# Four-layer forward and backward pass: attention's output stage inside the feed-forward loop, queries projected beside keys, backward weights transposed into SBUF

## The chip, the cores and the metric

One core of a Trainium2 chip runs the whole kernel. The metric is device time in microseconds, as the median of several runs; lower is better. A core has five engines with instruction queues of their own: TensorE (PE, matrix products, with a separate weight-load stream PEld), VectorE (DVE), ScalarE (ACT), GpSimd (POOL) and SyncE (SP), which here issues the DMA transfers. Each queue runs in its own order, and semaphores tie them to one another. Products land in PSUM, a small memory of eight banks, from which DVE or ACT must take them.

## The reference

The kernel computes the forward pass of four layers and the gradients for the input and all five weights. Shapes: sequence S = 2048, width D = 512, feed-forward width F = 1376, 32 heads of 16. Layers 0 and 2 are the linear attention A, layers 1 and 3 the gated feed-forward block B, with the same weights in both pairs.

```python
def _A_ref(x, wqkv, wo):                      # phi(t) = where(t>0, t+1, exp(t)) + 1e-6
    q, k, v = split(x @ wqkv)                 # each [32 heads, S, 16]
    pq, pk = phi(q), phi(k)
    kv = einsum("bhsd,bhse->bhde", pk, v)     # summed over the whole sequence
    z = einsum("bhsd->bhd", pk)               # the same
    num = einsum("bhqd,bhde->bhqe", pq, kv)
    den = einsum("bhqd,bhd->bhq", pq, z)[..., None] + 1e-6
    return (num / den).reshape(B, S, D) @ wo

def _B_ref(x, w_gate, w_up, w_down):
    return (sigmoid(x @ w_gate) * (x @ w_up)) @ w_down

x = x + _A_ref(layernorm(x)); x = x + _B_ref(layernorm(x))
x = x + _A_ref(layernorm(x)); x = x + _B_ref(layernorm(x))
```

Outputs are the last x and the gradients of its product with `grad_out`. What matters for the order of work: kv and z need the keys of every position, so no attention output can be computed before the last key; everything after them is independent from tile to tile.

## The kernel before

The sequence is cut into 16 tiles of 128 rows (`NST`), the width into 4 chunks of 128 (`NDC`), the feed-forward width into 11 chunks (the last of 96 rows), worked on in three slices of 512, 512 and 352 columns. The residual stream lives in SBUF in fp32 (`k.xs[st]`). DRAM buffers (`sv_...`) hold what the backward pass will need. The program is written as loops over tiles; a scheduler arranges each engine's queue from it, so a queue's order can differ from the program's.

*Start.* `load_stream` (L93) loads x in bf16, in batches of four tiles, and casts each tile to fp32, alternately on DVE and ACT. The weights follow in the same DMA queue.

*Attention, layers 0 and 2:* `a_fwd` (from L455). The layer norm of a tile (`layernorm_tile`, L290) is bn_stats and bn_aggr on DVE (L293, L295), rstd in two POOL steps (L296, L297), the factor nmr on DVE (L299) and the scaled copy on ACT (L300); four TensorE transposes (L308) and a copy out of PSUM follow. In the key pass, for each tile: project k (four products of 128x512, L484), phi (exp on ACT L490, a minimum L491 and a maximum L492 on DVE) into `pk_all`, and the accumulation of X = h^T phi(k) (L499) one tile later. Then z (L522), kv (L532, from X and the value weights, so v is never computed) and M = kv·wo (L537). In the query pass (`stage_q`), for each tile: project q (L484 again), phi, the product with z on POOL (`prod`, L553), its sum over heads on DVE (`den`, L555), a scalar step (L556), the reciprocal (L557), the normalised query `pqn` (L559, DVE), four transposes and an ACT copy. `stage_y`, four tiles behind (`LA = 4`), multiplies by M (L573), copies the result with ACT (L576) and adds it to x on POOL (L577). MT (L591) is computed and stored at the end, for the backward pass.

*Feed-forward, layers 1 and 3:* `b_fwd` (from L600). For each tile and slice: g (L652) and u (L655), four products each; sigmoid(g) and sigmoid(-g) on ACT (L657, L659); hh = u · sigmoid on DVE (L660); a second product on POOL (L661) for the backward pass; and transposes of the slice before (L617) with ACT copies (L620, L622). One tile behind, `finish` runs 11 products with the down weights (L629), a DVE add to x (L631), and the next layer's norm for that tile (`nxt.stage`), or, in layer 3, a copy of the output (`out_cb`, L191).

*Weights for the backward pass.* `wT_groups` (L336) transposes the weights in groups of four PE transposes with an evacuation on DVE or ACT. The groups run as `extra` at the end of each tile: 34 groups (gate, up, down) in layer 1, 16 (wqkv, wo) in layer 3. All go through a staging tile into DRAM. `load_b_weights` (L205) loads them back ahead of each B layer's backward pass.

*Backward.* `b_bwd_p1` and `a_bwd_p1` walk the layers down, with passes for weight gradients behind them. In layer 3 `GPrep` casts the incoming gradient into `k.xs` (L704, L706) and transposes it. In `a_bwd_p1` the gradient of z is accumulated by small products `dz` (L971) that need `cneg_bf` from POOL (L969).

Of the kernel before, what the change touches and what calls it, by code (L numbers as in the profile page):

```python
# [17 lines left out]
D = 512  # L18
# [32 lines left out]
def kernel(  # L51
# [41 lines left out]
    def load_stream(io, src2d, b):  # L93
        stg_t = io.tile([P, NB, D], BF16, name="io_in")
        if b == 0:
            nc.sync.dma_start(out=stg_t[:, 0, :], in_=src2d[0:P, :])
            nc.sync.dma_start(out=stg_t[:, 1:NB, :],
                              in_=src2d[P:NB * P, :].rearrange("(n p) d -> p n d", p=P))
        else:
            nc.sync.dma_start(out=stg_t[:], in_=dram_batch(src2d, b))  # L100
        for j in range(NB):
            st = b * NB + j
            if j % 2 == 0:
                nc.vector.tensor_copy(k.xs[st][:], stg_t[:, j, :])
            else:
                nc.scalar.copy(k.xs[st][:], stg_t[:, j, :])
        return stg_t
    k.load_stream = load_stream

    def store_stream(io, dst2d, b):  # L110
        stg_t = io.tile([P, NB, D], BF16, name="io_out")
        for j in range(NB):
            st = b * NB + j
            nc.gpsimd.tensor_scalar(stg_t[:, j, :], k.xs[st][:], 1.0, 0.0, ALU.mult, ALU.add)
        nc.sync.dma_start(out=dram_batch(dst2d, b), in_=stg_t[:])
    k.store_stream = store_stream


    k.sv = {}
    for l in range(4):  # L120
# [18 lines left out]
        wgT=dram.tile([F, D], BF16, name="wgT_d"),  # L139
        wuT=dram.tile([F, D], BF16, name="wuT_d"),  # L140
# [11 lines left out]
    k.A_wo = A_wo  # L152
    with tc.tile_pool(name="wfwd", bufs=1) as wfwd:
        k.wqkv = wfwd.tile([P, NDC, 3 * D], BF16, name="wqkv")
        with tc.tile_pool(name="io0", bufs=2) as io:
            load_stream(io, x_in, 0)
            nc.sync.dma_start(out=k.wqkv[:], in_=A_wqkv.rearrange("(c p) j -> p c j", p=P))
            for b in range(1, NST // NB):
                load_stream(io, x_in, b)
# [9 lines left out]
        nc.sync.dma_start(out=k.wd[0:FLAST, NFC - 1, :], in_=B_w_down[(NFC - 1) * P:F, :])  # L169

        with ExitStack() as lctx:
            k.lnres = dict(
                stg=lctx.enter_context(tc.tile_pool(name="ln_stg", bufs=2)),
                hT=lctx.enter_context(tc.tile_pool(name="ln_hT", bufs=4)),
                small=lctx.enter_context(tc.tile_pool(name="ln_small", bufs=6)),
                ps=lctx.enter_context(tc.tile_pool(name="ln_ps", bufs=1, space=PSUM)),
            )
            k.hres = lctx.enter_context(tc.tile_pool(name="ln_hall", bufs=1))
            lns = [FwdLNAll(k, l) if l % 2 == 0 else FwdLN(k, l) for l in range(4)]
            wtg_b, wtg_a = wT_groups(k)  # L180
            a_fwd(k, 0, lns[0], nxt=lns[1])
            with tc.tile_pool(name="wt_stage", bufs=2) as wt_stage:
                b_fwd(k, 1, lns[1], nxt=lns[2], extra=wtg_b, wt_stage=wt_stage)
            a_fwd(k, 2, lns[2], nxt=lns[3])
            ostg = lctx.enter_context(tc.tile_pool(name="out0_stg", bufs=2))
            ocur = {}

            def out_cb(st):
                if st % NB == 0:
                    ocur["t"] = ostg.tile([P, NB, D], BF16, name="out0_t")  # L190
                nc.scalar.copy(ocur["t"][:, st % NB, :], k.xs[st][:])  # L191
                if st % NB == NB - 1:
                    nc.sync.dma_start(out=dram_batch(out0, st // NB), in_=ocur["t"][:])
            with tc.tile_pool(name="wt_stage2", bufs=2) as wt_stage:
                b_fwd(k, 3, lns[3], out_cb=out_cb, extra=wtg_a, wt_stage=wt_stage)
# [5 lines left out]
    with ExitStack() as bctx:  # L201
        wb = bctx.enter_context(tc.tile_pool(name="wbwd", bufs=1))
        k.wb = wb

        def load_b_weights():  # L205
            k.wdT = wb.tile([P, NDC, F], BF16, name="wdT", tag="w_c")
            nc.sync.dma_start(out=k.wdT[:], in_=k.wT["wdT"].rearrange("(c p) f -> p c f", p=P))
            k.wuT = wb.tile([P, NFC, D], BF16, name="wuT", tag="w_a")
            k.wgT = wb.tile([P, NFC, D], BF16, name="wgT", tag="w_b")
            for t_sb, t_d in ((k.wuT, k.wT["wuT"]), (k.wgT, k.wT["wgT"])):  # L210
                nc.sync.dma_start(out=t_sb[:, 0:NFC - 1, :],
                                  in_=t_d[0:(NFC - 1) * P, :].rearrange("(c p) j -> p c j", p=P))
                nc.sync.dma_start(out=t_sb[0:FLAST, NFC - 1, :], in_=t_d[(NFC - 1) * P:F, :])
# [76 lines left out]
def layernorm_tile(k, small, x_t, h_out, rstd_out):  # L290
    nc = k.nc
    stats = small.tile([P, 6], F32, name="ln_stats")
    nc.vector.bn_stats(stats[:], x_t[:])  # L293
# [5 lines left out]
    nc.vector.tensor_scalar(nmr[:], mv[:, 0:1], -1.0, rstd_out, ALU.mult, ALU.mult)  # L299
    nc.scalar.activation(h_out, x_t[:], ACT.Identity, bias=nmr[:], scale=rstd_out)  # L300


def transpose_blocks(k, ps_pool, dst, src_blocks, evac, tag="tp"):
    nc = k.nc
    n = len(src_blocks)
    ps = ps_pool.tile([P, n, P], BF16, name=tag, tag=tag)
    for i, sb in enumerate(src_blocks):
        nc.tensor.transpose(ps[:, i, :], sb, k.ident[:])  # L308
    evac_copy(k, dst, ps[:], evac)
# [26 lines left out]
def wT_groups(k):  # L336
    nc = k.nc
    groups, groups_a = [], []
    cnt = [0]

    def evac(dst, src):
# [4 lines left out]
        cnt[0] += 1  # L346

    for w_sb, wT_d, C in ((k.wg, k.wT["wgT"], F), (k.wu, k.wT["wuT"], F),
                          (k.wqkv, k.wT["wqkvT"], 3 * D), (k.wo, k.wT["woT"], D)):
        ncc = (C + P - 1) // P  # L350
        for cc0 in range(0, ncc, 4):
            ccs = list(range(cc0, min(cc0 + 4, ncc)))
            holder = {}
            for j, cc in enumerate(ccs):
                def g(stage, ps_pool, w_sb=w_sb, wT_d=wT_d, C=C, cc0=cc0, ccs=ccs, j=j, cc=cc, holder=holder):
                    if j == 0:
                        holder["t"] = stage.tile([P, 4, D], BF16, name="wt_st")
                    st_t = holder["t"]
                    r = min(P, C - cc * P)
                    ps = ps_pool.tile([P, NDC, P], BF16, name="hhT_ps")  # L360
                    for rc in range(NDC):
                        nc.tensor.transpose(ps[0:r, rc, :], w_sb[:, rc, cc * P:cc * P + r], k.ident[:])
                    evac(st_t[0:r, j, :], ps[0:r, :, :].rearrange("p a b -> p (a b)"))
                    if j == len(ccs) - 1:
                        nfull = len([c_ for c_ in ccs if min(P, C - c_ * P) == P])
                        if nfull > 0:
                            nc.sync.dma_start(
                                out=wT_d[cc0 * P:(cc0 + nfull) * P, :].rearrange("(n p) d -> p n d", p=P),
                                in_=st_t[:, 0:nfull, :])
                        if nfull < len(ccs):  # L370
                            c_ = ccs[nfull]
                            r_ = C - c_ * P
                            nc.sync.dma_start(out=wT_d[c_ * P:c_ * P + r_, :], in_=st_t[0:r_, nfull, :])
                (groups_a if w_sb is k.wqkv or w_sb is k.wo else groups).append(g)
    for cc in range(NDC):
        holder = {}
        for fs in range(3):
            def g(stage, ps_pool, cc=cc, fs=fs, holder=holder):
                if fs == 0:
                    holder["t"] = stage.tile([P, F], BF16, name="wdt_st")  # L380
                st_t = holder["t"]
                fcs = fchunks_of_slice(fs)
                ps = ps_pool.tile([P, NDC, P], BF16, name="hhT_ps")
# [4 lines left out]
                evac(st_t[:, c0:c0 + w], ps[:].rearrange("p a b -> p (a b)")[:, 0:w])  # L388
                if fs == 2:
                    nc.sync.dma_start(out=k.wT["wdT"][cc * P:(cc + 1) * P, :], in_=st_t[:])  # L390
            groups.append(g)
    return groups, groups_a
# [5 lines left out]
class FwdLN:  # L398
# [7 lines left out]
    def stage(self, st):  # L406
# [7 lines left out]
        layernorm_tile(k, R["small"], k.xs[st], h_t, k.rstd[l][:, st:st + 1])  # L414
# [3 lines left out]
        transpose_blocks(k, R["ps"], hT[:], [h_t[:, c * P:(c + 1) * P] for c in range(NDC)], "vector", tag="ln_tp")  # L418
# [11 lines left out]
class FwdLNAll:  # L430

    def __init__(self, k, l):
        self.k, self.l = k, l
# [3 lines left out]
    def stage(self, st):  # L437
# [3 lines left out]
        R = k.lnres  # L441
        if st == 0:
            self.h_all = k.hres.tile([P, NST, D], BF16, name="h_all")
            self.hT_all = k.hres.tile([P, NST, NDC, P], BF16, name="hT_all")
        h_t = self.h_all[:, st, :]
        layernorm_tile(k, R["small"], k.xs[st], h_t, k.rstd[l][:, st:st + 1])
        transpose_blocks(k, R["ps"], self.hT_all[:, st, :, :], [h_t[:, c * P:(c + 1) * P] for c in range(NDC)],
# [729 lines left out]
```

## Time and profile before

| | us |
|---|---|
| median of 3 runs (1398.99 to 1402.82) | 1399.81 |
| the profiled execution's own time | 1402.44 |
| its span (first to last instruction) | 1400.6 |
| PE busy / DVE / ACT / POOL | 1244.4 / 712.8 / 591.1 / 339.6 |
| mean granted TensorE clock | 0.965 |

The profile shows one execution. In its lines "L652" is a line of the kernel, "128x512" partitions by elements, "x4" the number of instructions in the line. A bracket such as [20.43 <-DMA ssd_ld] is the idle time of that engine before the instruction and what ended it. TensorE instructions are pipelined, so one of 128x512 has a duration of 379 ns while the next follows after 216.

Landmarks on this execution's clock, from its timeline:

| event | us |
|---|---|
| first key projection of layer 0 | 14.0 |
| z of layer 0 complete | 53.9 |
| first g product of layer 1 | 124.9 |
| last y product of layer 1 | 276.4 |
| z of layer 2 complete | 310.4 |
| first g product of layer 3 | 383.3 |
| last y product of layer 3 | 521.1 |
| first transposes of the backward pass | 541.5 |
| end | 1400.6 |

### The profile page before, as it was taken

To read this page: it belongs to the slowest core of one execution; us is meant where nothing else is said; L and a number is where in the kernel's file an instruction comes from. 1 tells how busy PE (TensorE), PEld (TensorE's weight loads), DVE (VectorE), ACT (ScalarE), POOL (GpSimd) and SP (SyncE) were. 2 spreads that over 40 slices of the span, in tenths; PEclk is the share of its full clock that TensorE was granted. 3 is DMA by queue.
4 is the path that set the end of the run, shared out by engine and by line. 5 is a ranking of instruction groups with operands and counts; after the bars stand their busy time and mean duration, and the time that the engine had idled before them with its cause. 6 is when DMAs were issued, how large, how long until landed. Compare 5 with 4: busy or idle time off the path is not lost. (4 is left out here: it accounts for less than half of the span.)

```text
span 1400.6 us, 22220 instructions
## 1 busy us (share of the span) xinstructions
PE 1244.4 (89%) x8506; PEld 720.3 (51%) x8628; DVE 712.8 (51%) x1440; ACT 591.1 (42%) x1092; POOL 339.6 (24%) x500
## 2 busy tenths in 40 slices
PE   5867999896689985999978999999999989996998
PEld 2423555442245542555454557775455745554777
DVE  6694655558853332666476660016555285650211
ACT  7445666634467652444442441134443333520000
POOL 4175444406753330000162000001100441110000
PEclk9988999999899996999999999999999999998999
DMA  8312444421234459755673739887554956559963
GB/s 316 135 61 99 182 183 187 168 105 61 86 146 192 167 187 314 271 176 177 199 224 106 240 100 319 223 224 245 200 187 168 297 155 190 182 142 313 254 159 91
DMA packets 260937, 260.15 MB, mean 186 GB/s; under 512 B 28448, under 2 KB 241376, under 8 KB 260832
## 3 DMA queue, kind: packets, MB, share of 16 engines
q1 hardware_dynamic: 248352, 251.40, 56.1%
q10 hardware_dynamic: 12480, 7.34, 1.9%
q8 instruction: 67, 1.10, 0.3%
q14 instruction: 38, 0.31, 0.1%
HBM read 139.85 MB, written 118.85 MB: 185 GB/s over the span
## 5 line engine op out<-in xcount | busy, mean ns | idle before, releaser
L868 PE MATMUL p_ps<-p_set,p_a 128*128 128x256 bf16 (+1 forms) x1792 | 194.6, 267 | 10.5 <-DVE dw_stg L873 7.4
L868 PEld LDWEIGHTS <-p_a 128*128 128x128 bf16 x1792 | 161.3, 99 | 33.6 <-issue 6.5
L661 POOL TENSOR_TENSOR ssd_t<-hh_t,oms 128x512 bf16<-128x512 bf16 (+1 forms) x96 | 101.7, 1062 | 99.6 <-ACT oms L659 60.1
L765 ACT COPY ddT<-T_ps 128x1024 bf16<-128x1024 bf16 (+1 forms) x96 | 83.2, 867 | 93.1 <-PE T_ps L763 92.9
L683 DVE SCALAR_TENSOR_TENSOR junk<-t_sb,h_ld 128x512 bf16<-128x512 f32 x64 | 45.8, 715 | 139.8 <-ACT t_sb L681 139.7
L685 POOL TENSOR_SCALAR ab<-c 128x2 f32<-128x2 f32 x64 | 12.2, 191 | 384.2 <-DVE junk L683 373.9
L777 PEld LDWEIGHTS <-ddT 128*128 128x128 bf16 (+1 forms) x704 | 65.9, 97 | 68.9 <-issue 10.4
L777 PE MATMUL dh_ps<-wuT,ddT 128*128 128x512 bf16 (+1 forms) x330 | 94.4, 379 | 6.9 <-ACT t_sb L681 3.4
L652 PE MATMUL g_ps<-wg,hT 128*128 128x512 bf16 (+1 forms) x368 | 92.9, 362 | 8.1 <-ACT oms L659 5.2
L681 ACT ACTIVATE t_sb<-dh_ps,rstd_all 128x512 f32<-128x512 f32 x64 | 44.0, 687 | 133.0 <-issue 60.4
L660 DVE TENSOR_TENSOR hh_t<-u_ps,ssd_t 128x512 bf16<-128x512 f32 (+1 forms) x96 | 60.8, 633 | 67.0 <-PE u_ps L655 49.5
L655 PE MATMUL u_ps<-wu,hT 128*128 128x512 bf16 (+1 forms) x384 | 93.0, 361 | 0.0
L795 PE MATMUL dhh_ps<-wdT,gT 128*128 128x512 bf16 x383 | 87.2, 364 | 2.8 <-ACT gT L317 2.8
L797 DVE TENSOR_TENSOR dd_t<-dhh_ps,ssd_ld 128x512 bf16<-128x512 f32 (+1 forms) x96 | 60.5, 630 | 53.9 <-issue 48.7
L484 PE MATMUL mm_ps<-wqkv,hT_all 128*128 128x512 bf16 x249 | 73.0, 409 | 14.2 <-DVE pq_t L492 13.9
L777 PE MATMUL dh_ps<-wgT,ddT 128*128 128x512 bf16 (+1 forms) x352 | 81.3, 379 | 0.0
L898 PE MATMUL p_ps<-p_a,p_set 128*128 128x512 bf16 (+1 forms) x331 | 79.0, 379 | 2.5 <-DMA p_set<-sv_hdd 2.0
L629 PE MATMUL y_ps<-wd,hhT 128*128 128x512 bf16 (+1 forms) x336 | 78.3, 379 | 1.2 <-DVE x L631 0.4
L620 ACT COPY hhT<-hhT_ps 128x512 bf16<-128x512 bf16 (+1 forms) x96 | 49.5, 516 | 57.9 <-PE hhT_ps L617 57.9
L763 PEld LDWEIGHTS <-dd_t 128*128 128x128 bf16 (+1 forms) x704 | 50.7, 100 | 40.6 <-DVE dd_t L797 18.9
L763 PE MATMUL T_ps<-ident,dd_t 128*128 128x128 bf16 (+1 forms) x704 | 66.5, 220 | 3.5 <-DVE dd_t L797 3.2
L553 POOL TENSOR_TENSOR prod<-pq_t,zb 128x512 bf16<-128x512 bf16 x32 | 43.3, 1357 | 93.5 <-DVE pq_t L492 90.1
(193 smaller groups left out, 2250.1 us busy)
## 6 DMA issues: line engine op xcount, KB each, us to landing
p_set<-sv_hdd SPq DMA_DIRECT2D x30, 1024.0 KB, 7.5
sv_ssd<-ssd_t SPq DMA_DIRECT2D x32, 688.0 KB, 3.0
ssd_ld<-sv_ssd SPq DMA_DIRECT2D x32, 688.0 KB, 5.6
sv_hdd<-dd_t SPq DMA_DIRECT2D x32, 688.0 KB, 3.8
sv_hdd<-hh_t SPq DMA_DIRECT2D x32, 344.0 KB, 2.2
h_ld<-sv_h SPq DMA_DIRECT2D x32, 256.0 KB, 3.7
p_a<-sv_h SPq DMA_DIRECT2D x12, 512.0 KB, 6.7
sv_h<-h_all SPq DMA_DIRECT2D x8, 512.0 KB, 3.6
```

The costliest lines, as they stand in the source:

```text
L484: nc.tensor.matmul(ps[:], lhsT=ln.hT_all[:, st, kc, :], rhs=k.wqkv[:, kc, n * D:(n + 1) * D], start=(kc == 0), stop=(kc == NDC - 1))
L629: nc.tensor.matmul(y_ps[:], lhsT=T["hhT"][0:r, fc, :], rhs=k.wd[0:r, fc, :], start=(fc == 0), stop=(fc == NFC - 1))
L652: nc.tensor.matmul(g_ps[:, 0:w], lhsT=hT[:, kc, :], rhs=k.wg[:, kc, c0:c0 + w], start=(kc == 0), stop=(kc == NDC - 1))
L655: nc.tensor.matmul(u_ps[:, 0:w], lhsT=hT[:, kc, :], rhs=k.wu[:, kc, c0:c0 + w], start=(kc == 0), stop=(kc == NDC - 1))
L660: nc.vector.tensor_tensor(hh_t[:, c0:c0 + w], u_ps[:, 0:w], ssd_t[:, 0, c0:c0 + w], ALU.mult)
L661: nc.gpsimd.tensor_tensor(ssd_t[:, 1, c0:c0 + w], hh_t[:, c0:c0 + w], oms[:, 0:w], ALU.mult)
L763: nc.tensor.transpose(tps[0:r, a, i, :], dd[:, a, fc * P:fc * P + r], k.ident[:])
L765: nc.scalar.copy(ddT[:, :, fcs[0]:fcs[0] + nfull, :], tps[:, :, 0:nfull, :])
L777: nc.tensor.matmul(dh_ps[:], lhsT=T["ddT"][0:r, a, fc, :], rhs=wT[0:r, fc, :], start=(i == 0), stop=(i == n_mm - 1))
L795: nc.tensor.matmul(dhh_ps[:, 0:w], lhsT=gT[:, jc, :], rhs=k.wdT[:, jc, c0:c0 + w], start=(jc == 0), stop=(jc == NDC - 1))
L868: nc.tensor.matmul(psv[:, icl, :], lhsT=lhs_all[:, st, ic * P:(ic + 1) * P], rhs=set_t[:, st, 0:W], start=(st == 0), stop=(st == NST - 1))
L898: nc.tensor.matmul(ps[0:r, :], lhsT=st_t[:, st, j * P:j * P + r], rhs=g_all[:, st, :], start=(st == 0), stop=(st == NST - 1))
```

## The change

The key and query passes become one: `kq_fwd` projects k and q for a tile one after the other, takes both exponentials into one tile, and does the minimum for both in one DVE instruction of twice the width. phi(q) of all tiles stays in SBUF (`pq_all`). The transposes of h move from the layer norm into this pass (ACT copies them), the X accumulation runs two tiles behind, and MT is computed right after M. The phi(q) factor is stored tile by tile instead of in batches of four.

The rest of attention moves into the feed-forward loop, `ab_fwd`. `front1` (the product with z, den), `front2` (scalar, reciprocal, pqn) and `front3` (transposes) run three tiles ahead of the feed-forward tile (`FLAG`), `attn_y` and its add two tiles ahead (`YLAG`). The attention add moves from POOL, behind an ACT copy, to DVE, straight from PSUM. Attention's y and the feed-forward's y share one PSUM bank; the transposes of pqn and of h share another.

x stays in bf16 for layer 0 (no casts; the first attention add reads it), and wqkv is loaded in three parts between the batches of x. nmr moves from DVE to POOL. The weight groups change places: 16 (wqkv, wo) run in layer 1, 34 (down, up, gate) in layer 3, and these are evacuated straight into the SBUF tiles that layer 3's backward pass reads, with one store each to DRAM for layer 1's; so layer 3 has no reload. The incoming gradient is read in bf16 where it is used. The `dz` products are issued one tile later in the program.

```diff
 def layernorm_tile(k, small, x_t, h_out, rstd_out):
-    nc.vector.tensor_scalar(nmr[:], mv[:, 0:1], -1.0, rstd_out, ALU.mult, ALU.mult)
+    nc.gpsimd.tensor_scalar(nmr[:], mv[:, 0:1], -1.0, rstd_out, ALU.mult, ALU.mult)
...
-            load_stream(io, x_in, 0)
-            nc.sync.dma_start(out=k.wqkv[:], in_=A_wqkv.rearrange("(c p) j -> p c j", p=P))
+        nc.sync.dma_start(out=x_bf[:, 0, :], in_=x_in[0:P, :])
+        nc.sync.dma_start(out=k.wqkv[:, :, D:2 * D], in_=wq_src[:, :, D:2 * D])
...
+        k.ps = {nm: lctx.enter_context(tc.tile_pool(name=f"fw_ps_{nm}", bufs=n, space=PSUM))
+                for nm, n in (("t", 2), ("g", 2), ("u", 2), ("y", 1), ("ln", 1))}
...
+def kq_fwd(k, aq, l, ln):
+        def mm_tile():
+            nm = "tty"[cnt[0] % 3]
...
+        for st in range(NST):
+            ln.ensure(st + 3)
+            ps_k = proj(st, 1)
+            ps_q = proj(st, 0)
+            e_t = work.tile([P, 2, D], BF16, name="e_t", bufs=2)
+            nc.scalar.activation(e_t[:, 0, :], ps_k[:], ACT.Exp)
+            nc.scalar.activation(e_t[:, 1, :], ps_q[:], ACT.Exp)
+            a_t = work.tile([P, 2, D], BF16, name="a_t")
+            nc.vector.tensor_scalar(a_t[:], e_t[:], 1.0, EPS, ALU.min, ALU.add)
+            nc.vector.scalar_tensor_tensor(pk_all[:, st, :], ps_k[:], 1.0 + EPS, a_t[:, 0, :], ALU.add, ALU.max)
+            nc.vector.scalar_tensor_tensor(A.pq_all[:, st, :], ps_q[:], 1.0 + EPS, a_t[:, 1, :], ALU.add, ALU.max)
+            nc.sync.dma_start(out=sv["phq"][rows(st), :], in_=a_t[:, 1, :])
+            stage_hT(st + 2)
...
+            if st >= XLAG:
+                accum_X(st - XLAG)
...
+FLAG = 3
+YLAG = 2
+def ab_fwd(k, A, ln, nxt=None, out_cb=None, extra=(), x_src=None):
+        def front1(st):
+            prod = work.tile([P, D], BF16, name="prod", bufs=2)
+            nc.gpsimd.tensor_tensor(prod[:], A.pq_all[:, st, :], A.zb[:], ALU.mult)
+            den = small.tile([P, H], F32, name="den")
+            nc.vector.tensor_reduce(den[:], prod[:].rearrange("p (h e) -> p h e", h=H), AX.X, ALU.add)
...
+        def front2(st):
+            nc.vector.tensor_scalar(den[:], den[:], EPS, None, ALU.add)
+            nc.vector.reciprocal(A.rden_all[:, st, :], den[:])
+            nc.vector.tensor_tensor(f["pqn"].rearrange("p (h e) -> p h e", h=H),
+                                    A.pq_all[:, st, :].rearrange("p (h e) -> p h e", h=H),
+                                    A.rden_all[:, st, :].unsqueeze(2).to_broadcast([P, H, DH]), ALU.mult)
...
+        def front3(st):
+            pqnT = stg.tile([P, NDC, P], BF16, name="pqnT", bufs=3)
+            transpose_blocks(k, k.ps["ln"], pqnT[:], [f["pqn"][:, c * P:(c + 1) * P] for c in range(NDC)],
+                             "scalar", tag="ln_tp")
...
+        def attn_y(st):
+            y_ps = k.ps["y"].tile([P, D], F32, name="y_ps")
+            for c in range(NDC):
+                nc.tensor.matmul(y_ps[:], lhsT=pqnT[:, c, :], rhs=A.M_sb[:, c, :],
+                                 start=(c == 0), stop=(c == NDC - 1))
+            res = k.xs[st][:] if x_src is None else x_src[:, st, :]
+            nc.vector.tensor_tensor(k.xs[st][:], y_ps[:], res, ALU.add)
...
+        for st in range(FLAG):
+            front1(st)
+            front2(st)
+            front3(st)
+            if st >= 1:
+                attn_y(st - 1)
+                ln.stage(st - 1)
...
-                if fs >= 1:
+                if fs == 0:
+                    attn_y(st + YLAG)
+                    front1(st + FLAG)
+                else:
                     transposes(T, fs - 1)
+                if fs == 1:
+                    front2(st + FLAG)
             if prev is not None:
                 finish(prev)
+            front3(st + FLAG)
             transposes(T, 2)
...
+def wT_groups_b(k, wb):
+                evac(k.wdT[:, cc, c0:c0 + w], ps[:].rearrange("p a b -> p (a b)")[:, 0:w])
+                if cc == NDC - 1 and fs == 2:
+                    nc.sync.dma_start(out=k.wT["wdT"].rearrange("(c p) f -> p c f", p=P), in_=k.wdT[:])
...
 def b_bwd_p1(k, l):
-    k.load_b_weights()
+    if k.g_from_input != l:
+        k.load_b_weights()
...
-                for c in range(NDC):
-                    nc.tensor.matmul(dz_ps[:, c, :], lhsT=pqn_st[:, c * P:(c + 1) * P],
-                                     rhs=cneg_bf[:, c * 8:(c + 1) * 8], start=False, stop=(st == NST - 1),
-                                     skip_group_check=True)
+                if dzq:
+                    accum_dz(*dzq.pop())
+                dzq.append((st, cneg_bf))
```

## The prediction

> **What bounds the kernel now.** I first cut the span into its stages and read the busy time of each engine in each one. The rows below give: stretch, length, busy us (and instructions) of PE, PEld, DVE, ACT and POOL, granted clock, DMA share, GB/s. The stretches are: layer 0's key pass, its query and output stage, layer 1's feed-forward loop, layer 2's key pass, its query stage, layer 3's loop, and the gap ahead of the backward pass.
>
> ```profile
> 14.00:54.00 40.00, 37.97 (x201) 18.28 (x203) 25.19 (x67) 27.70 (x48) 8.19 (x21) 1.00 0.75 266
> 54.00:125.00 71.00, 47.66 (x238) 20.48 (x240) 57.53 (x113) 32.14 (x56) 44.37 (x38) 0.86 0.18 64
> 125.00:276.00 151.00, 143.70 (x964) 76.51 (x980) 81.78 (x192) 102.55 (x206) 71.80 (x104) 0.99 0.47 179
> 276.00:310.00 34.00, 32.43 (x146) 14.10 (x148) 19.27 (x40) 12.50 (x20) 0.78 (x2) 1.00 0.27 95
> 310.00:383.00 73.00, 47.63 (x246) 20.76 (x249) 60.96 (x129) 34.73 (x60) 47.86 (x48) 0.86 0.20 72
> 383.00:521.00 138.00, 130.54 (x828) 71.66 (x844) 57.12 (x112) 94.09 (x193) 58.28 (x65) 0.98 0.44 168
> 521.00:541.00 20.00, 0.09 (x1) 0.00 (x0) 0.69 (x1) 0.62 (x1) 0.00 (x0) 0.59 1.08 344
> ```
>
> Key passes and loops are TensorE's: PE is busy for 95% of them. The two query stages are not. PE is busy for 47.7 of 71 and 47.6 of 73 us, at a granted clock of 0.86, and DVE is the busy engine (57.5 and 61.0). The list of DVE's groups in the first of these stages says with what (busy us, then mean ns):
>
> ```profile
> L559 DVE TENSOR_TENSOR pqnstage<-pq_t,rden_all 128x512 bf16<-128x512 bf16 x16 | 14.3, 895 | 0.0
> L555 DVE TENSOR_REDUCE den<-prod 128x32 f32<-128x512 bf16 x16 | 10.9, 681 | 5.5 <-POOL prod L553 5.5
> ...
> L556 DVE TENSOR_SCALAR den<-den 128x32 f32<-128x32 f32 x16 | 7.8, 488 | 0.0
> L557 DVE RECIPROCAL rden_all<-den 128x32 f32<-128x32 f32 x16 | 5.4, 339 | 0.0
> ```
>
> Together the normalisation costs DVE .90+.68+.49+.34 = 2.4 us a tile, and PE waits on it. The third place is the gap: the weights' reload stands ahead of the first gradient in SP's queue, and the first backward transposes wait 20.4 us for loads (start, duration, instruction).
>
> ```profile
> 529.37 0.65 SPq L211 DMA_DIRECT2D wgT<-wgT_d  x1
> 530.06 3.63 SPq L213 DMA_DIRECT2D wgT<-wgT_d  x1
> 533.80 0.37 SPq L701 DMA_DIRECT2D gstage<-in_grad_out_dram  x1
> ...
> 541.53 0.59 PE L308 MATMUL gT_ps<-ident,gstage 128*128 128x128 bf16 x4 [20.43 <-DMA ssd_ld<-sv_ssd]
> ```
>
> From 541.5 to the end (859.1 us) the queues stay nearly as they were.
>
> **Landmarks before:** first projection 14.0, layer 0's z done 53.9, first g of layer 1 124.9, last y 276.4, layer 2's z 310.4, first g of layer 3 383.3, last y 521.1, first backward transpose 541.5. I put each in the changed kernel in turn.
>
> **1. Keys and queries in one pass, layer 0.** Casts of x go; each of the 16 tiles gains the query projection (.865 us of PE by the matmul interval of .216) and four transposes (.22), and loses no PE work. The first projection still waits for POOL's first layer norms, near 14. In the new queue DVE does all 16 bn_stats (.674 each, 10.8 us) before its first phi, so I put that at 17 and the second query projection at 18.4. From there PE needs 12 × .216 + .22 = 2.81 us a tile. But three PSUM slots turn for two products a tile, so a tile's query projection waits until the tile before has released its key slot: projection 1.03, exp .60, the merged minimum .55 (.29 for half the width, nearly doubled), max .69, hand-overs .13: 3.0 us, which is what I take (2.81 to 3.6; the upper one with the minimum twice the .506 that the query stage shows). Tile 15's query starts at 18.4 + 14 × 3.0 + 2 (ACT's copies of the transposes lag) = 62.4; its phi (1.03+.6+.55+2×.69 = 3.6) and the last X and z (2.5) give z at 68.5, 14.6 later than before.
>
> **2. From z to the first g.** Before 71.0 and 73 us. Now zb, X copies, kv and M take 5.7 us (the same operations took as much before). The first prod shares a pool that waits for layer 0's MT store, issued then and landing 3.4 us later: 9.3 with the hand-over. In POOL's new queue eight prods (1.36 each, 10.9) stand ahead of the first tile's rstd; behind them a chain add .69, bn .67, aggr .17, rstd, pow and nmr 1.0, h .82, transposes .40, copy .58 = 4.3, with queues on DVE 5.8. Sum 26. Bounds: 14 (one tile's own chain from zb: prod 1.36, den .68+.17+.34, pqn .90, transposes and copy 1.0, y 1.03, then 4.3, with .3 for each of 14 hand-overs), and 30 (four den scalars at 1.07, as at 65.10 us, rather than the .17 of 64.16). First g: 94.5.
>
> **3. The merged loop.** Layer 3's loop now repeats every 8.09 us without a gap, one group of four transposes (.22) in it: 7.87 a tile. Layer 1 after: 16 × 7.87 + 14 attention products × .865 + 13 transposes of pqn × .22 + 16 weight groups × .22 = 144.4; layer 3 has 34 groups: 148.4. Three things come on top.
> First, DVE is behind in the first three tiles: its queue there holds some 9 pqn, 10 den chains, 9 hh, 3 finishing adds and bn's, 32 us by the rows above against 25 of PE: +8 in both layers (0 to 12).
> Second, in layer 1 the next layer's norm is in PE's order. Its chain now reads:
>
> ```profile
> 168.27 0.69 DVE L631 TENSOR_TENSOR x<-y_ps,x 128x512 f32<-128x512 f32 x1 [1.71 <-PE y_ps L629]
> ...
> 170.65 0.22 POOL L296 TENSOR_SCALAR rstd_all<-ln_mv 128x1 f32<-128x1 f32 x1 [3.10 <-DVE ln_mv L295]
> ...
> 171.55 0.21 DVE L299 TENSOR_SCALAR ln_nmr<-ln_mv,rstd_all 128x1 f32<-128x1 f32 x1
> 171.80 0.81 ACT L300 ACTIVATE h_all<-x,ln_nmr,rstd_all 128x512 bf16<-128x512 f32 x1 [0.79 <-DVE ln_nmr L299]
> ...
> 172.67 0.40 PE L308 MATMUL ln_tp<-ident,h_all 128*128 128x128 bf16 x4 [0.25 <-ACT h_all L300]
> ```
>
> 4.4 us from add to transposes, of which 3.53 lie up to ACT. The new queues put tile st+2's transposes ahead of the second slice's u, about 3.9 us of PE work behind that add, and hold two norms between the add and the ACT step, with pqn (.90) and prod (1.36) in front of them: 1.2 us late, for some 11 tiles: +13 (0 to 25). What is queued behind the waiting transposes is the rest of PE's stream; sigmoids and hh wait with it. Moving nmr to POOL (.21 on DVE; .22 there) saves one hand-over and adds to POOL, 0. Layer 3 has no second norm and no such wait.
> Third, the last tile drains: +2. Loops: 167 (before 151.5) and 159 (137.8). The adds moved from POOL to DVE (.69 a tile) are covered while DVE has room: per tile hh 1.9, two adds 1.4, two norms 1.7, normalisation 2.4, a copy .4 = 7.8 of 9.2. Uncovered, each would cost its .69.
>
> The Trainium skill, page "SBUF — State Buffer", section "Who interferes with whom", speaks against this merge: a DVE operation with two SBUF inputs or in a two-port mode and a GpSimd operation exclude one another, and the loser stands for the whole instruction. The row agrees in kind: the den scalar took 0.17 us at 64.16 and 1.07 at 65.10, during a POOL add of 1.26. By the rule, if pqn and the den scalar each met a whole prod, the loops would lose 2 × 1.36 a tile, 87 us; by the rows, whose means were taken with POOL busy 44 of 71 us, they are already in the sum.
>
> **4. Layer 2.** The pass starts at 261.5, has its first phi after 5.2 us (the last tile's norm), then 14 × 3.0 + 6.1: z at 314.8. First g at 340.8 by step 2, last y at 499.8.
>
> **5. Weights straight to SBUF.** 34 groups move from layer 1 to layer 3: their transposes are counted in step 3. Six reload issues leave the head of SP's queue, but the stores of wgT (1.4 MB) and of the output stay ahead of the gradient: 9.5 us, between 5 (issue and landing alone, 3.4 rounded up with transposes' wait) and 15 (a reload's share left). First backward transpose: 509.3. Casts of the gradient (.62 on ACT, .43 on DVE) leave the start; hidden behind loads, 0 to 1. The dz products stay at the same places in PE's queue, so their 10.8 us of waits for POOL stay: 0 (3 at most).
>
> **Sum.** 541.5 − 509.3 = 32.2 us of gain. The profiled execution had 1402.4 with a span of 1400.6 (so 1370 and 1368 after); on the median of 1399.8 that is **1368**.
>
> **The rivals.** B, the loop covers everything: prologues at 15 (−22), no norm stall in layer 1 (−13): 1333. For it: PE's order leaves slices between each producer and its consumer. Against: POOL's eight prods stand in a queue that nothing reorders.
> C, the vector engines bound it: the merged minimum at 1.01 (+.46 × 28 = 13) and prologues at 30 (+8): 1389. For it: .506 against .29 for the same operation in the two stages. Against: in the one-pass stage POOL has only the norms.
> D, slower: the single y bank. Attention's y and the finishing y now hand one PSUM bank over twice a tile, each time through a DVE add. If hh (.69) and pqn (.90) stand before one of the two adds, PE loses 1.6 us a tile: 32 × 1.6 = 51, 1419. It decides from 1.0 us a tile, where it eats the 32. Against: the add came 1.7 us after DVE fell idle in the row above.
> E, parts do not do what they say: the gap stays at 20 because the wgT store takes the reload's place: +10, 1378, inside the forecast's own range.
>
> **How the numbers follow.** Forecast with E, 1350 to 1382: .50. B .22, C .16, D .08, and .04 for a gain that lands within 0.3% (4 us), about what a measurement of this kernel can tell from no change. Faster .88, same .04, slower .08. The range 1330 to 1392 leaves out the lower half of B, D and part of the last.
>
> **What would show it.** Right: first g near 94 and 341; one-pass tiles at 3.0; loops of 167 and 159 with waits of the norm's transposes in layer 1 only; a gap of 9 to 10. Wrong: waits of y on the add (D), of PE on the merged minimum (C), POOL not at the end of the prologue's chain (B), or a backward pass that is not 859 us long.

## The result and the profile after

The changed kernel takes **1379.85 us** (median of 4 runs, 1376.80 to 1386.05) against 1399.40 for the kernel before, measured beside it: a ratio of 0.9861, 95% interval 0.9823 to 0.9899. That is 1.4% faster. The profiled execution has a span of 1377.7 us, 22.9 less than before.

The same landmarks as before, each in the profiled execution, with what the prediction had for it:

| stage | before | predicted | after |
|---|---|---|---|
| first z complete | 53.9 | 68.5 | 70.8 |
| from there to layer 1's first g | 71.0 | 26 | 25.1 |
| layer 1's loop, first g to last y | 151.5 | 167 | 175.3 |
| from there to layer 2's z | 34.0 | 53.3 | 53.2 |
| from there to layer 3's first g | 73 | 26 | 25.0 |
| layer 3's loop | 137.8 | 159 | 160.1 |
| gap to the first backward transpose | 20.4 | 9.5 | 10.4 |
| the rest | 859.1 | 859.1 | 857.8 |

The busy time by stage, in the same columns as in the prediction (stretch, length, busy us and instructions of PE, PEld, DVE, ACT and POOL, granted clock, DMA share, GB/s), cut at the new landmarks:

```profile
15.00:70.80 55.80, 52.44 (x269) 24.51 (x268) 31.64 (x61) 35.42 (x62) 11.07 (x31) 1.00 0.64 225
70.80:96.00 25.20, 9.34 (x62) 5.02 (x60) 17.34 (x35) 4.81 (x9) 10.38 (x12) 0.63 0.18 63
96.00:271.20 175.20, 151.90 (x973) 80.28 (x972) 99.52 (x201) 107.64 (x213) 92.54 (x146) 0.98 0.36 139
271.20:324.40 53.20, 50.19 (x271) 23.82 (x270) 29.83 (x53) 30.27 (x53) 1.36 (x4) 1.00 0.37 131
324.40:349.40 25.00, 9.24 (x62) 4.90 (x60) 17.25 (x35) 4.80 (x9) 10.97 (x14) 0.68 0.18 64
349.40:509.40 160.00, 153.57 (x1038) 84.15 (x1036) 92.60 (x180) 106.29 (x222) 77.16 (x101) 0.99 0.42 160
509.40:519.90 10.50, 0.08 (x2) 0.05 (x2) 3.19 (x5) 0.62 (x1) 0.00 (x0) 0.73 1.02 341
```

The two query stages with an idle third of PE are gone; in their place stand two short stretches of 25 us in which PE works for 9. The passes are PE's (94%), and so is layer 3's loop (96%). Layer 1's loop is the exception: 23 us without PE. The list of waits in it (engine and line, what it waited for, us in total, times, longest) names most of them:

```profile
PE ln_tp L287 <- ACT hstage L279: 20.9, 13, 3.1
...
ACT h_all L279 <- POOL ln_nmr L278: 18.2, 15, 1.8
...
ACT hstage L279 <- POOL ln_nmr L278: 6.6, 4, 2.2
```

PE waits 20.9 us for the normalised tile that it is to transpose, once in nearly every iteration. The timeline of one iteration shows the chain (start, duration, instruction):

```profile
185.50 0.69 DVE L654 TENSOR_TENSOR x<-y_ps,x 128x512 f32<-128x512 f32 x1 [2.00 <-PE y_ps L652]
...
186.22 1.29 DVE L272 BATCH_NORM_STATS2 ln_stats<-x 128x6 f32<-128x512 f32 x2
...
187.69 0.22 POOL L275 TENSOR_SCALAR rstd_all<-ln_mv 128x1 f32<-128x1 f32 x1 [3.20 <-DVE ln_mv L274]
...
189.16 0.81 ACT L279 ACTIVATE h_all<-x,ln_nmr,rstd_all 128x512 bf16<-128x512 f32 x1 [0.94 <-POOL ln_nmr L278]
...
189.75 0.27 POOL L278 TENSOR_SCALAR ln_nmr<-ln_mv,rstd_all 128x1 f32<-128x1 f32 x1
...
190.06 0.81 ACT L279 ACTIVATE hstage<-x,ln_nmr,rstd_all 128x512 bf16<-128x512 f32 x1
...
190.93 0.40 PE L287 MATMUL ln_tp<-ident,hstage 128*128 128x128 bf16 x4 [1.40 <-ACT hstage L279]
```

Two norms run as a pair ("x2" of bn_stats at 186.22): one of the tile just finished, for layer 2, and one of the tile to which attention was added an iteration earlier, for layer 1's own next product. The second had its input some 7 us before (its attention add stands at 177.96), but it comes behind the finishing add in DVE's queue, and behind the other norm in POOL's and ACT's. PE's transposes need the second one.

### The profile page after: what moved, and what is told of

Read it like the earlier page. It is cut to its first block, busy times and chain, and to the rows that moved or that the text cites. A ratio compares the mean times of both kernels' runs of the same rounds, so it can differ in the third digit from the quotient of the medians.

```text
span 1377.7 us, 22244 instructions
## 1 busy us (share of the span) xinstructions
PE 1234.0 (90%) x8628; PEld 719.4 (52%) x8628; DVE 700.1 (51%) x1344; ACT 568.6 (41%) x1060; POOL 313.9 (23%) x534
## 5 line engine op out<-in xcount | busy, mean ns | idle before, releaser
L811 PEld LDWEIGHTS <-ddT 128*128 128x128 bf16 (+1 forms) x704 | 66.0, 97 | 69.3 <-issue 10.5
L683 PE MATMUL g_ps<-wg,hT 128*128 128x512 bf16 (+1 forms) x384 | 96.6, 366 | 0.0
L832 DVE TENSOR_TENSOR dd_t<-dhh_ps,ssd_ld 128x512 bf16<-128x512 f32 (+1 forms) x96 | 60.5, 630 | 57.2 <-issue 49.8
L830 PE MATMUL dhh_ps<-wdT,gT 128*128 128x512 bf16 (+1 forms) x384 | 87.0, 362 | 2.5 <-ACT gT L296 2.5
L933 PE MATMUL p_ps<-p_a,p_set 128*128 128x512 bf16 (+1 forms) x352 | 83.6, 379 | 1.4 <-DMA p_set<-sv_hdd 1.4
L652 PE MATMUL y_ps<-wd,hhT 128*128 128x512 bf16 (+1 forms) x352 | 81.6, 380 | 0.2 <-DVE x L654 0.2
L908 DVE TENSOR_TENSOR dw_stg<-p_ps,dw_stg 128x512 bf16<-128x512 f32 (+1 forms) x32 | 20.6, 648 | 87.8 <-PE p_ps L903 64.5
L688 ACT ACTIVATE ssd_t<-g_ps 128x512 bf16<-128x512 f32 (+1 forms) x96 | 53.1, 553 | 27.3 <-PE g_ps L683 26.8
L833 DVE TENSOR_TENSOR dd_t<-dhh_ps,ssd_ld 128x512 bf16<-128x512 f32 (+1 forms) x96 | 60.1, 626 | 0.0
```

The source lines that it names most:

```text
L652: nc.tensor.matmul(y_ps[:], lhsT=T["hhT"][0:r, fc, :], rhs=k.wd[0:r, fc, :], start=(fc == 0), stop=(fc == NFC - 1))
L683: nc.tensor.matmul(g_ps[:, 0:w], lhsT=hT[:, kc, :], rhs=k.wg[:, kc, c0:c0 + w], start=(kc == 0), stop=(kc == NDC - 1))
L811: nc.tensor.matmul(dh_ps[:], lhsT=T["ddT"][0:r, a, fc, :], rhs=wT[0:r, fc, :], start=(i == 0), stop=(i == n_mm - 1))
L830: nc.tensor.matmul(dhh_ps[:, 0:w], lhsT=gT[:, jc, :], rhs=k.wdT[:, jc, c0:c0 + w], start=(jc == 0), stop=(jc == NDC - 1))
L832: nc.vector.tensor_tensor(dd[:, 0, c0:c0 + w], dhh_ps[:, 0:w], ssd[:, 0, c0:c0 + w], ALU.mult)
L933: nc.tensor.matmul(ps[0:r, :], lhsT=st_t[:, st, j * P:j * P + r], rhs=g_all[:, st, :], start=(st == 0), stop=(st == NST - 1))
```

## The experiments

All runs are of the changed kernel with one edit, except where edits are put together. The first is the changed kernel itself, as the measure.

**The changed kernel again.** 

> The changed kernel once more, as the measure for the other runs on the same chip: a ratio to the kernel before of 0.985 (0.981 to 0.990), layer 1's loop 175 us from the first g to the last y, layer 3's 160.

Measured: 1380.89 us, ratio 0.9859 (0.9832 to 0.9886), span 1377.3; loops 173.4 and 159.8. The stages of the forward pass repeat within some 2 us. Whole executions scatter more: the eight of this kernel on record have spans from 1375.1 to 1384.6 us. And the time from the last y of layer 3 to the end lies between 866.2 and 872.6 us in the profiles of all runs of this record that hold the change, most of it code that no edit touches. So a difference in a stage is read from the profiles, and a difference of a few us between medians is not given to an edit unless a stage shows it.

**Norm started early.** The norm is split from its transposes, and called in the iteration that adds attention to the tile:

```diff
+            ln.norm(st + YLAG)
             if prev is not None:
                 finish(prev)
             front3(st + FLAG)
```

> The norm of the tile whose attention y was just added is started in the same iteration, ahead of the finishing add; its transposes stay one iteration later. Theory (in layer 1 the two norms stand as a pair behind the finishing add in DVE's and POOL's queues, and PE's transposes wait for the second of them): the waits of the norm's transposes for ACT's copy in layer 1 fall from 20.9 us to under 3, layer 1's loop from 175 to 152-157 us, layer 3's stays within 2 us of 160, and the time falls by 18 to 23 us. Rival (the loop is short of DVE time, 99.5 us busy of 175, and of POOL time, 92.5, and the transposes are only where the delay shows): the wait moves to another instruction, the loop stays above 168 and the time falls by under 8.

Measured: 1360.41 us, ratio 0.9706 (0.9691 to 0.9720), 20.5 us less than the run above. Layer 1's loop takes 155.9 us, layer 3's 159.9. In layer 1's loop PE no longer waits for the norm's ACT copy at all. The stage line of that loop, in a window that ends 0.9 us behind its last y:

```profile
95.10:252.00 156.90, 148.35 (x958) 80.24 (x973) 99.97 (x203) 106.33 (x214) 92.61 (x146) 0.99 0.41 156
```

DVE and POOL are as busy as before in us (99.97 and 92.61), in a loop 17 to 19 us shorter. So their time did not bound the loop: their order did.

**MT's tile kept.** `MT_sb` is allocated in the pool that outlives the pass, not in the one whose memory the loop takes over:

```diff
-        MT_sb = big.tile([P, NDC, D], BF16, name="MT_sb")
+        MT_sb = aq.tile([P, NDC, D], BF16, name="MT_sb")
```

> MT's tile lies in memory that the feed-forward loop does not take over, so the first product with z needs no landing of its store. Theory of the prediction (eight products on POOL and the first tile's norm follow the start of the first product): the first product starts 4 to 5 us earlier after z in both layers, the first g too, 8 to 10 us in all. Rival (the copies of M and MT on DVE, and the attention y that needs M, set the first g): under 5 us in all.

In the changed kernel, the timeline from layer 2's z (324.4) to the first g reads:

```profile
333.12 5.58 POOL L596 TENSOR_TENSOR prod<-pq_all,zb 128x512 bf16<-128x512 bf16 x5 [8.05 <-DMA sv_MT<-MT_sb]
...
338.66 0.68 DVE L608 TENSOR_TENSOR pqnstage<-pq_all,rden_all 128x512 bf16<-128x512 bf16 x1
...
343.42 0.68 DVE L632 TENSOR_TENSOR x<-y_ps,x 128x512 f32<-128x512 f32 x1
...
345.73 0.23 POOL L275 TENSOR_SCALAR rstd_all<-ln_mv 128x1 f32<-128x1 f32 x1 [0.73 <-DVE ln_mv L274]
...
349.38 1.06 PE L683 MATMUL g_ps<-wg,hT 128*128 128x512 bf16 x2
```

Measured: 1372.76 us, ratio 0.9797 (0.9782 to 0.9811), 8.1 us less than the changed kernel again. The stretch from z to the first g shrinks from 25 to 20.2 us in both layers: POOL's 8 us of waiting for a store to land were worth 5 a layer. The lines also speak against the other half of the prediction's account: at 345.73 POOL waits for DVE, so its products are not what holds up the first norm.

**The reload put back.** `load_b_weights` is called for layer 3 as well.

```diff
-    if k.g_from_input != l:
-        k.load_b_weights()
+    k.load_b_weights()
```

> Layer 3's backward weights are loaded again from DRAM, as before the change, though the transposes have already put them into SBUF. Theory (the reload's issues and bytes stand ahead of the first gradient): the gap from the last y to the first backward transpose grows from 10.5 to 19-22 us and the time by 9 to 11. Rival (the gap is the wait for the last output's store, which hides the reload): 13 us at most, and the time grows by under 3.

Measured: 1385.48 us, ratio 0.9889 (0.9873 to 0.9906); the gap is 13.6 us against 10.0. The theory's gap of 19 to 22 us did not come, and the rival's 13 is passed by 0.6. The time itself decides less: the medians differ by 4.6 us, the profiled spans by 1.8, and the intervals overlap. SP's issues around the gap show why the gap grows so little:

```profile
507.92 0.39 SPq L178 DMA_DIRECT2D out_dram<-out_t  x1
...
510.76 0.36 SPq L192 DMA_DIRECT2D wgT<-wgT_d  x1
511.62 0.69 SPq L738 DMA_DIRECT2D gstage<-in_grad_out_dram  x1
```

Of the reloads only the one of wgT is issued here; those of wdT and wuT went out inside the loop (419.4 and 467.8). The gradient's issue still comes 3.7 us behind that of the last output, as without the reload (514.52 behind 510.87, shown further down), and it is the load itself that lands later. Before the change all five issues (the prediction counted six) stood in this place, from 522.97 to 533.7.

**The merge undone.** The 16 fronts, attention products and adds run ahead of the loop, which holds none of them:

```diff
-        for st in range(FLAG):
+        for st in range(NST):
             front1(st)
             front2(st)
             front3(st)
             if st >= 1:
                 attn_y(st - 1)
-                ln.stage(st - 1)
+        attn_y(NST - 1)
...
-                    attn_y(st + YLAG)
-                    front1(st + FLAG)
```

> The merge alone undone: the fronts, attention products and adds of all 16 tiles run between z and the first g, the feed-forward loop holds none of them; the one-pass keys and queries, the weights in SBUF and all else stay. Theory (the gain is the merge: DVE's normalisation costs time only where PE has nothing else): from z to the first g 60 to 70 us instead of 25 (16 times 3.1 us of DVE, the wait for MT's store and one tile's chain), loops of 146-150 and 140-144 us instead of 174 and 160, so 30 to 38 us slower than the changed kernel and 10 to 18 slower than the kernel before. Rival (the one pass and the weights bring the gain, the merge gives back in the loops what it saves ahead of them): within 12 us of the changed kernel.

Measured: 1393.25 us, ratio 0.9942 (0.9922 to 0.9961): 12 to 13 us slower than the changed kernel, just past the rival's 12 and far from the theory's 30 to 38. The stage lines (z to g, loop of layer 1, loop of layer 3):

```profile
69.90:121.60 51.70, 27.60 (x169) 12.90 (x170) 43.98 (x92) 13.79 (x24) 23.57 (x25) 0.87 0.17 61
121.60:280.90 159.30, 132.98 (x848) 71.06 (x862) 70.17 (x143) 97.48 (x198) 78.53 (x132) 0.99 0.37 143
385.80:523.20 137.40, 134.47 (x911) 74.97 (x924) 60.10 (x119) 100.35 (x207) 63.55 (x88) 1.00 0.46 175
```

My expectation was off at both ends. The stage takes 51.7, not 60 to 70: without the query's phi and with POOL less busy, DVE needs 44 us for it. And layer 1's loop takes 159 although it holds no attention work: the wait for the norm's transposes is there too:

```profile
PE ln_tp L287 <- ACT hstage L279: 25.2, 13, 2.3
```

So the merge takes 26.7 us out of the stage and puts 14 to 16 us back into layer 1's loop and 22.6 into layer 3's, which is about the PE work that moves (14 products and 13 transposes, 15 us) plus, in layer 3, the crowded first tiles: there the first y product comes 18.7 us into the loop instead of 14.0, the next two tiles take 11.81 and 10.32, and the rest settle near 9.62. The wait for the norm belongs not to the merge but to the norm's chain.

The queues show why the first tiles are crowded. The program puts one front into each iteration, but in the changed kernel's layer 1 the last of the 16 products with z starts at 123.7, 28 us into a loop of 175, while the attention adds go on to 242.4: the scheduler has run the products far ahead of the tiles that need them.

Against the kernel before, this run also shows what the rest of the change is worth without the merge. Its span is 9.1 us shorter: 10.5 in the gap and 5.3 in the attention layers are gained, 7.8 are lost in layer 1's loop.

**The gradient loaded early.** The first two tiles of the gradient go into a tile of their own, loaded ahead of layer 3's loop.

```diff
+            k.gpre = keep.tile([P, 2, D], BF16, name="gpre")
+            nc.sync.dma_start(out=k.gpre[:], in_=dram_batch(g_in, 0, 2))
```

> The first two tiles of the incoming gradient are loaded ahead of layer 3 into memory of their own. Theory (the gap waits for the landing of the last output's store, whose memory the gradient's tile takes over): the first backward transpose comes within 2 us of the last y instead of 10, and the time falls by 4 to 8 us, not by the whole 8 to 9, since the second operand of the next step is loaded behind the same store. Rival (the loads behind it take its place): the time falls by under 2.

In the changed kernel the gradient's load is issued when the last output's store has landed:

```profile
510.87 0.39 SPq L178 DMA_DIRECT2D out_dram<-out_t  x1
...
514.52 0.37 SPq L738 DMA_DIRECT2D gstage<-in_grad_out_dram  x1
...
519.88 0.58 PE L287 MATMUL gT_ps<-ident,gstage 128*128 128x128 bf16 x4 [10.42 <-DMA gstage<-in_grad_out_dram]
```

Measured: 1376.80 us, ratio 0.9823 (0.9800 to 0.9847); the interval overlaps that of the changed kernel, and the span is 1376.8 against 1377.3. The transposes now come 3.6 us before the last y, but the list of waits shows the store again, one step on:

```profile
PE dhh_ps L834 <- ACT gT L298: 6.0, 1, 6.0
...
ACT gT L298 <- DMA out_dram<-out_t: 4.0, 1, 4.0
```

ACT's copy of the transposes goes into memory that the same store still reads. The wait moved. What it is worth shows one step further: the first DVE product with the gradient (`dd_t`) starts 10.8 us behind the last y, against 13.7 and 13.3 in the two profiles of the changed kernel. That is a gain of some 2.5 to 3 us at that point, between the two accounts. At the end of the kernel it can't be told from the scatter.

**nmr back on DVE,** in all layers:

```diff
-    nc.gpsimd.tensor_scalar(nmr[:], mv[:, 0:1], -1.0, rstd_out, ALU.mult, ALU.mult)
+    nc.vector.tensor_scalar(nmr[:], mv[:, 0:1], -1.0, rstd_out, ALU.mult, ALU.mult)
```

> The norm's factor nmr goes back from POOL to DVE; all else as changed. Prediction's step: 0, one hand-over against a busy queue; within 3 us of the changed kernel. Rival (POOL's queue of two norms is what makes the transposes of layer 1 late, 0.27 us a norm): the waits of 21 us fall by a third or more and the time by 6 or more.

Measured: 1373.34 us, ratio 0.9798 (0.9772 to 0.9823), clear of the changed kernel's. PE's wait for the norm in layer 1 falls to 11.8 us and the loop to 164.6, as the rival has it. But the first z comes at 75.9, 5 later. The wait in layer 1's loop:

```profile
PE ln_tp L287 <- ACT hstage L279: 11.8, 14, 2.4
```

DVE's timeline at the start shows the price:

```profile
10.07 0.21 DVE L278 TENSOR_SCALAR ln_nmr<-ln_mv,rstd_all 128x1 f32<-128x1 f32 x1 [0.89 <-POOL rstd_all L276]
10.59 0.21 DVE L278 TENSOR_SCALAR ln_nmr<-ln_mv,rstd_all 128x1 f32<-128x1 f32 x1 [0.31 <-POOL rstd_all L276]
```

Between the bn_stats of the first 16 tiles, DVE now waits for POOL's rstd, tile by tile, 4.9 us in 12 waits, and its first minimum for phi comes at 23.18 instead of 19.39.

**nmr by layer:** on POOL in layer 0, on DVE in the others.

```diff
+    eng = nc.gpsimd if l == 0 else nc.vector
...
-    nc.gpsimd.tensor_scalar(nmr[:], mv[:, 0:1], -1.0, rstd_out, ALU.mult, ALU.mult)
+    eng.tensor_scalar(nmr[:], mv[:, 0:1], -1.0, rstd_out, ALU.mult, ALU.mult)
```

> nmr on POOL in layer 0 only, on DVE in layers 1 to 3; all else as changed. Theory (nmr on POOL saves 5 us at the start, where DVE would wait for POOL's rstd between its 16 bn_stats, and costs 9 us in layer 1's loop): the first z as in the changed kernel (70.8), layer 1's loop 163-167 us, 1367 to 1372 us. Rival (the shorter loop of the run with nmr on DVE throughout came from its later start): layer 1's loop above 171, no gain over the changed kernel.

Measured: 1369.20 us, ratio 0.9762 (0.9732 to 0.9791), first z at 70.4, layer 1's loop 162.9. Both halves of the account hold: nmr on POOL saves 5 us at the start and costs 10 in layer 1's loop.

**Three edits together:** norm early, MT kept, gradient early.

> The norm started early, MT's tile kept, and the gradient loaded early, together. If the three act in different stages, their gains add: 20 for the norm, 6 to 8 for MT, 4 to 8 for the gradient, so 1346 to 1352 us, a ratio of 0.960 to 0.965 to the kernel before. If the earlier start of the loops is eaten by DVE's backlog in the first tiles, 1355 or more.

Measured: 1352.88 us, ratio 0.9646 (0.9620 to 0.9671), inside the expected ratio and 0.9 us above the expected time. In the forward pass the parts add: loops of 157.0 and 159.4, stretches of 20.2 in both layers. The gradient's early load again brings `dd_t` to 11.2 us behind the last y, but the time from the last y to the end is 870.7 us, against 870.1 in the changed kernel again, so its share does not show in the total.

**den in one buffer,** on top of the three:

```diff
-            den = small.tile([P, H], F32, name="den")
+            den = small.tile([P, H], F32, name="den", bufs=1)
```

> The three edits together, and den in one buffer instead of four, so that DVE's queue can't hold the sums of later tiles ahead of the first attention add. Theory (what is left of the stretch from z to the first g is DVE's queue: six sums and three normalised queries stand ahead of the first add where two or three are needed): the stretch falls from 20.2 to 16.5-18.5 us in both layers, the time by 3 to 7 us from 1352.9. Rival (POOL's products, as the prediction has it, or PE's own work at its lower clock, set it): within 1 us of 20.2.

Measured: **1345.42 us**, ratio 0.9583 (0.9554 to 0.9612), the fastest of all. The stretch from z to the first g is 17.3 us in both layers, in the range that DVE's order gives and outside the rival's. DVE's sums up to the first attention add of layer 0, in the three edits together:

```profile
76.05 1.27 DVE L609 TENSOR_REDUCE den<-prod 128x32 f32<-128x512 bf16 x2
...
77.98 0.69 DVE L609 TENSOR_REDUCE den<-prod 128x32 f32<-128x512 bf16 x1
...
82.27 1.26 DVE L609 TENSOR_REDUCE den<-prod 128x32 f32<-128x512 bf16 x2
...
84.21 0.69 DVE L609 TENSOR_REDUCE den<-prod 128x32 f32<-128x512 bf16 x1
84.81 0.68 DVE L643 TENSOR_TENSOR x<-y_ps,x_bf 128x512 f32<-128x512 f32 x1
```

and with den in one buffer:

```profile
76.31 0.68 DVE L609 TENSOR_REDUCE den<-prod 128x32 f32<-128x512 bf16 x1
...
78.69 0.67 DVE L609 TENSOR_REDUCE den<-prod 128x32 f32<-128x512 bf16 x1
...
81.06 0.67 DVE L609 TENSOR_REDUCE den<-prod 128x32 f32<-128x512 bf16 x1
81.87 0.69 DVE L643 TENSOR_TENSOR x<-y_ps,x_bf 128x512 f32<-128x512 f32 x1
```

Three sums instead of six stand ahead of the add, which comes 5.6 us behind the first sum instead of 8.8: with fewer buffers the scheduler can't put the sums of later tiles ahead of it. Of the 7.5 us between the medians the order explains less than half. In the profiles the last y of layer 3 comes 3.5 us earlier (6 in the two stretches, with layer 1's loop 2 us longer); the rest lies behind it, in code that the edit does not touch.

**nmr by layer, with all of this:**

> The run before with nmr on DVE in layers 1 to 3. With the norm started early the second norm is no longer on PE's path, so nmr's engine should not matter: within 3 us of the run before. If POOL's time still bounds layer 1's loop (92.6 of 157 us busy), it is 4 us or more faster.

Measured: 1352.58 us, ratio 0.9636 (0.9611 to 0.9662): 7 us slower than the run before, which neither account foresaw. The loops take 161.2 and 162.2 instead of 158.9 and 159.7. The lists of waits from 90 to 247 us, in layer 1's loop, first of this run, then of the run before:

```profile
DVE ln_nmr L281 <- POOL rstd_all L279: 19.5, 28, 1.5
...
PE t_ps L652 <- DVE hh_t L703: 7.2, 7, 2.2
```

```profile
PE t_ps L651 <- DVE hh_t L702: 1.8, 2, 0.9
```

DVE stands waiting for POOL's rstd, and PE waits longer for DVE's hh. Once PE no longer waits for the norm, the hand-over on DVE delays DVE's other work, and POOL is the better place. The two loops account for 4.8 us of the 7.

## Why the prediction was right or wrong

**Right: where the time goes, stage by stage.** Faster, with four of the seven stages within 1 us, layer 3's loop within 1.1 and the first z within 2.3. The query stages gave up 46 and 48 us, the loops grew by the PE work that moved, and the backward pass behind the gap kept its length within 1.3 us (the dz products' wait is 10.8 us before and after, as the unchanged order of PE's queue said).

**Wrong in size: the gain,** 22.9 us between the profiled spans instead of 32.2 (19.5 between the medians). The sum of the misses is z +2.3, the two stretches −1.9, layer 1's loop +8.3, layer 3's +1.1, the rest −0.1 and +0.9: +10.6, less 1.3 in the backward pass. One term carries it: the second of the three things on top of layer 1's loop, the norm's wait. It was put at 1.2 us for 11 tiles, 13 in all; it measured 20.9, in 13 waits. The loop's other terms hold: 175.3 − 20.9 = 154.4, which is 144.4 + 8 + 2. The range of 0 to 25 given for the term held it. Its mechanism holds in one half: the chain does hold two norms between the finishing add and ACT's copy. The other half does not: the term also put a pqn and a prod in front of them, and in the iteration shown neither stands there. DVE idles 2.00 us ahead of the add and POOL 3.20 ahead of the first rstd. What stands in front of the second norm is the other norm of the pair, and taking the pair apart ends the wait.

The first z's 2.3 us are lost at the start: DVE's first minimum for phi came at 19.39 instead of 17 and the second query projection at 21.73 instead of 18.4, while the 14 steps behind it took 42.9 us instead of 44. Three slips in the working are small beside this: layer 3's terms add up to 158.4, not 159; the backlog of 32 us against 25 is 7, not 8; and the one-pass tile with a minimum of 1.01 comes to 3.46 us, not 3.6.

**Wrong in kind: "adds to POOL, 0" for nmr.** The step weighed 0.21 us on DVE against 0.22 on POOL. What it costs is its place in a queue that holds two norms: on POOL the first norm's nmr, .27 long, stands before the second norm's next step, and the second norm comes later. PE's wait in layer 1's loop was 20.9 us with nmr on POOL, and 11.8 and 12.2 in the two runs with it on DVE. At the start it is the reverse, by 5 us, and with the norm started early DVE is again the worse place, by 4.8 in the two loops (7 between the medians). There is no single price.

**Right in length, wrong in cause: from z to the first g.** 26 was forecast and 25 came, but half of the working was wrong. The wait for MT's store is as described (8.05 us; kept apart, it gives back 5). Eight prods do stand ahead of the first rstd in POOL's queue (five from 333.12, three from 341.63), but they do not set its time: POOL idles 2.92 us ahead of the last three and 0.73 ahead of rstd, each time for DVE, which works through sums and queries of later tiles. One buffer for den took 3 us off. It also left five prods instead of eight ahead of that rstd, but in both runs POOL was idle for DVE there (0.73 and 1.02 us in layer 3).

**Right in length, wrong in cause: the gap.** 9.5 forecast, 10.4 came. The prediction had the stores of wgT and of the output stay ahead of the gradient in SP's queue. The trace has three parts instead: 1.4 us to the issue of the last output's store, 3.65 until it has landed and the gradient's load is issued (its tile takes over memory that the store reads), and 5.4 for the gradient's own load. The reload put back cost 3.6, because only one of the three transposed weights is late. The other 6 us of the 10 saved against before stay saved in that run, in which wdT and wuT are reloaded inside the loop; before the change all issues stood behind it. That the weights' earlier memory and stores are the reason was not tried alone.

**The rivals.** B (loops cover everything) needs the norm's wait gone: the early norm makes that true, not the change. The sign named for it, POOL not at the end of the prologue's chain, did come, but with 25 us and not 15: DVE stood there. C needs a merged minimum of 1.01; it takes .43, below the .55 of the sum, and most one-pass tiles take 2.9 us (projections at 61.72 and 64.62). D: PE waited for the y bank 1.1 us in layer 1 and as much in layer 3, once each, ahead of the loop; inside the loops there is one such wait, of 0.2 us. E: the gap did not stay at 20.

**The rule weighed in the prediction** ("The Trainium skill", page "SBUF — State Buffer", section "Who interferes with whom"): pqn, a DVE operation with two SBUF inputs, took 710 ns on average with POOL busy 46% of the stage (the merge undone) and 895 with 63% (before). That agrees in kind, though the two stages differ in other things too. Single ones were stretched far more: up to 1436 ns in the changed kernel, against a median of 681. But no loss of such size shows on PE's path: layer 3's loop came out within 1.7 us of its terms' sum.

## What to carry to other kernels

Price a moved step by the queue that it joins, not by its duration: .2 us in front of a longer chain cost 10 in one loop, saved 5 in another place, and changed its sign once the chain was taken off the path. Where two chains of the same kind share three in-order engines, start each when its own input is ready; written together, they run as a pair, and both end when the later input comes. A buffer count is also an order: fewer buffers kept a scheduler from filling a queue with work that nobody yet needs.

## What was not expected of the hardware

POOL's product of 128x512 took 1357 ns on average in the kernel before and 1208 in the changed one (1461 and 1151 at the median), the same operation on the same shape; which work beside it makes the difference was not tried. Behind 10.3 us of an idle PE, with only two groups of transposes between, the attention product ran its four matmuls in 1.91 us instead of 1.03, and the granted clock of that stretch is 0.63; "The Trainium skill", page "TensorE: Matmul & The Clock Gate", section "What's actually happening", states a half-rate clock after an idle window of some 3.4 us, which this agrees with. In the fastest run the longest idle time ahead of the product is 3.19 us, and it still takes 1.89 at a granted clock of 0.77 over the stretch; how short an idle time is enough was not measured here.
